# A fused attention and MLP kernel: the prologue's steps in another order, with fewer zero products

## The chip, the cores and the metric

One core of one Trainium2 chip runs the program. The metric is the device time of one execution in microseconds, the median of the runs. The engines are PE (TensorE: matmuls, with the weight loads shown as PEld), DVE (VectorE), ACT (ScalarE), POOL (GpSimd) and SP, whose queue issues the DMAs.

## The reference

Attention over 4 batches, 8 heads, 768 positions and head size 64, in float32: each query sees the 31 keys nearest to it and 24 block summaries (the maximum of 32 keys, the mean of 32 values). Its output, as 3072 rows of 512, goes through a gated MLP with an inner size of 1536.

```python
scores_l = scale * np.matmul(q, k.transpose(0, 1, 3, 2))          # masked to |i - j| < 16
scores_s = scale * np.einsum('bhsd,bhnd->bhsn', q, k_sum) + np.log(32)
a = softmax over both, joined;  out = np.matmul(a, [v, v_sum])
g = x @ w_gate;  val = x @ w_val
return (g / (1 + np.exp(-g))) * val @ w_out
```

The MLP weights arrive as float64, two 32-bit words each.

## The kernel before

The 3072 rows are six blocks of 512 tokens (k = 0 to 5). A block's attention runs over four pairs of heads (u = 0 to 3), its MLP over twelve slices of the inner size (j = 0 to 11). For every float32 product of the MLP each operand is split into a high and a low part that PE multiplies at one pass each, so a slice is three groups of 12 matmuls of 128x512: `gate`, `val` (both line 647) and `down` (line 694).

**The steps.** Attention of (k,u): `sw` and `sp` (block 0) or `scores` (later blocks) are the score products, lines 472, 484 and 458; `ttr0`, `ttr1` take the masked maxima on DVE (line 505, the first half of the heads and the second); `exp0`, `exp1` run on ACT (521); `rcp` and `nrm` normalize (538, 539, 548 or 546); `tr0`, `tr1` turn the probabilities on PE (563); `pt0`, `pt1` copy them out of PSUM; `out` and `outp` multiply by the values (612 and 620); `split` and `rest` make the high and low part of the result (182 and 178). `keys` and `pool` take the block maxima of the keys (336), `pool_values` and `values` bring in the block means of the values (356; on PE the small product pv, line 394).

Weights of slice j (`gv` for gate and value weights together, `o` for the output weights, `g` and `v` apart for j = 0 and 11): `w_load` issues the DMA (201); `w_abs` on ACT (210) and `w_c1`, `w_c2`, `w_s1`, `w_s2` on DVE (215, 219, 227, 234) turn float64 into float32, each reading what the one before it wrote; `w_hi` (182 or 184) and `w_lo` (178) split it. In the MLP: `silu` (653, ACT), `mul` (658, DVE), `ah` (182) and `al` (178) make the split product that `down` reads.

**What sets the order.** The table PROLOGUE lists all 457 steps of block 0 (attention and MLP) and of block 1's attention. The program is built by reading it from the front, and dependencies without a semaphore keep every engine to that order. A step's suffix names its engine (`=a` ACT, `=d` DVE, `=p` POOL) or, for steps on PE, the PSUM pool of its bank (`y`, `g`: two banks each; `c`: four). A digit behind the pool letters asks for that many zero products of 128 columns in that bank ahead of the step (`zeros`, line 740). They change no result, since the step's own first product overwrites the bank. Blocks 2 to 5 and block 1's MLP follow in a loop that is not touched.

**Buffers that order the work.** `gate`, `val` and half of each `scores` share the two `g` banks, so each of them waits until the one two places before it has been read. `pro` holds block 0's tiles; `room(0)` closes it and opens the pools for block 1's tiles and the later weights in its place.

`w_lead` (line 193) shifts the weight tile of one slice by 24 words; `a_max` (line 489) allocates the probabilities when the first half is handled.

Of the kernel before, what the change touches and what calls it, by code (L numbers as in the profile page):

```python
# [100 lines left out]
kf(2) qf(2) qf(0) sw(0,2)=cc pool(2) sp(0,2) kf(0) ttr0(0,2) pool(0) exp0(0,2) ttr1(0,2) exp1(0,2)
sw(0,0)=yg2 sp(0,0) kq(1) kq(3) ttr0(0,0) pool(1) rcp(0,2) nrm(0,2)=p ttr1(0,0) exp0(0,0) w_load(0,g)
sw(0,1)=yg6 sp(0,1) w_load(1,gv) vr() ve() exp1(0,0) ttr0(0,1) vo() tr0(0,2)=c9 ttr1(0,1) rcp(0,0) w_abs(0,g)
exp1(0,1) w_c1(0,g) pool(3) exp0(0,1) w_c2(0,g) w_s1(0,g) w_abs(1,gv) rcp(0,1) tr1(0,2)=g sw(0,3)=cy4 sp(0,3)
ttr0(0,3) nrm(0,0)=p tr0(0,0)=c3 ttr1(0,3) exp0(0,3) exp1(0,3) pt0(0,2)=a w_s2(0,g) w_c1(1,gv) w_c2(1,gv)
rcp(0,3) tr1(0,0)=y nrm(0,1)=p tr0(0,1)=y1 w_s1(1,gv) tr1(0,1)=c nrm(0,3)=d w_s2(1,gv) fv()=g pt1(0,2)=a
w_load(0,v) out(0,2)=c pt0(0,0)=a fvc()=a outp(0,2) pt1(0,0)=a out(0,0)=c tr0(0,3)=c pt0(0,1)=a w_load(0,o)
w_abs(0,v) pt1(0,1)=a w_c1(0,v) w_hi(0,g)=a w_c2(0,v) w_abs(0,o) outp(0,0) tr1(0,3)=y w_lo(0,g)=d w_hi(1,gv)=a
w_s1(0,v) w_load(2,gv) w_c1(0,o) w_s2(0,v) w_load(3,gv) w_lo(1,gv)=d w_c2(0,o) out(0,1)=y split(0,0)=a rest(0,0)
w_s1(0,o) pt0(0,3)=a pt1(0,3)=a outp(0,1) w_abs(2,gv) split(0,1)=a w_load(1,o) cst() w_hi(0,v)=a out(0,3)=g outp(0,3)  # L110
room(0) rest(0,1) gate(0,0,0) split(0,2)=a gate(0,0,1) rest(0,2) gate(0,0,2) split(0,3)=a rest(0,3) w_c1(2,gv)
w_abs(3,gv) gate(0,0,3) gate(0,1) silu(0,0) w_c1(3,gv) w_c2(2,gv) w_s2(0,o) w_lo(0,v)=p w_s1(2,gv) w_c2(3,gv)
w_s2(2,gv) w_abs(1,o) val(0,0,0) val(0,0,1) silu(0,1) w_hi(0,o)=a val(0,0,2) w_s1(3,gv) w_c1(1,o) val(0,0,3)
load(1,0) val(0,1) w_hi(2,gv)=a w_lo(2,gv)=d w_load(2,o) w_c2(1,o) mul(0,0) ah(0,0)=a keys(1,0) gate(0,2)
w_abs(2,o) mul(0,1) w_lo(0,o)=d w_s1(1,o) al(0,0)=d ah(0,1)=a w_s2(3,gv) w_load(3,o) w_load(4,gv) silu(0,2)
scores(1,0) down(0,0) val(0,2) w_s2(1,o) w_hi(3,gv)=a al(0,1)=d ttr0(1,0) pool_values(1,0) ttr1(1,0)
w_lo(3,gv)=p w_abs(4,gv) w_abs(3,o) w_c1(4,gv) w_c1(2,o) w_c2(4,gv) gate(0,3) mul(0,2) val(0,3) w_load(5,gv)
w_s1(4,gv) w_c1(3,o) w_s2(4,gv) exp1(1,0) w_hi(1,o)=a w_c2(3,o) w_lo(1,o)=d exp0(1,0) w_hi(4,gv)=a w_s1(3,o)
w_c2(2,o) w_s2(3,o) w_s1(2,o) w_load(7,gv) w_load(6,gv) rcp(1,0) down(0,1) w_lo(4,gv)=d load(1,1) silu(0,3)
w_abs(5,gv) w_hi(3,o)=a w_c1(5,gv) mul(0,3) gate(0,4) val(0,4) ah(0,2)=a w_abs(7,gv) w_c2(5,gv) w_lo(3,o)=d  # L120
w_s1(5,gv) w_s2(2,o) nrm(1,0)=a w_hi(2,o)=a w_s2(5,gv) al(0,2)=d w_hi(5,gv)=a tr0(1,0) silu(0,4) w_abs(6,gv)
w_load(4,o) tr1(1,0) pt0(1,0)=a w_abs(4,o) w_lo(2,o)=d pt1(1,0)=a down(0,2) keys(1,1) mul(0,4) w_c1(6,gv)
w_lo(5,gv)=d w_c1(4,o) scores(1,1) ah(0,4)=a w_c2(6,gv) ah(0,3)=a ttr0(1,1) exp0(1,1) ttr1(1,1) al(0,4)=d
w_load(5,o) load_values(1,0) w_load(7,o) w_load(6,o) w_c1(7,gv) w_s1(6,gv) values(1,0)=a w_load(9,gv) gate(0,5)
al(0,3)=p w_abs(5,o) w_c2(4,o) w_s2(6,gv) w_load(8,gv) w_s1(4,o) val(0,5) w_c2(7,gv) w_hi(6,gv)=a down(0,3)
out(1,0) silu(0,5) w_lo(6,gv)=d w_s2(4,o) w_c1(5,o) w_s1(7,gv) gate(0,6) w_abs(6,o) mul(0,5) w_hi(4,o)=a
w_lo(4,o)=p down(0,4) pool_values(1,1) w_s2(7,gv) w_c2(5,o) load_values(1,1) exp1(1,1) w_c1(6,o) w_s1(5,o)
w_abs(7,o) w_abs(9,gv) w_c1(9,gv) w_c1(7,o) val(0,6) w_hi(7,gv)=a w_lo(7,gv)=d w_c2(9,gv) split(1,0)=a w_s2(5,o)
rcp(1,1) silu(0,6) w_abs(8,gv) w_c2(6,o) w_s1(9,gv) load(1,2) mul(0,6) rest(1,0) w_hi(5,o)=a w_c2(7,o) ah(0,5)=a
values(1,1)=a al(0,5)=p w_load(8,o) w_load(10,gv) w_s1(6,o) gate(0,7) silu(0,7) nrm(1,1)=a w_load(9,o) val(0,7)  # L130
w_c1(8,gv) w_lo(5,o)=d w_s2(9,gv) w_hi(9,gv)=a tr0(1,1) down(0,5) mul(0,7) ah(0,7)=a pt0(1,1)=a keys(1,2)
scores(1,2) pool_values(1,2) tr1(1,1) w_lo(9,gv)=d w_s2(6,o) w_abs(8,o) w_s1(7,o) gate(0,9) ttr0(1,2) ttr1(1,2)
pt1(1,1)=a w_c2(8,gv) out(1,1) ah(0,6)=a load(1,3) w_hi(6,o)=a w_lo(6,o)=d exp0(1,2) al(0,6)=p w_s2(7,o)
w_c1(8,o) exp1(1,2) w_hi(7,o)=a w_s1(8,gv) al(0,7)=d w_s2(8,gv) w_c2(8,o) val(0,9) down(0,6) w_lo(7,o)=d
w_abs(10,gv) w_abs(9,o) w_c1(9,o) w_hi(8,gv)=a w_c1(10,gv) w_lo(8,gv)=d down(0,7) silu(0,9) rcp(1,2) w_c2(10,gv)
w_s1(10,gv) mul(0,9) split(1,1)=a w_s2(10,gv) w_c2(9,o) nrm(1,2)=a gate(0,8) tr0(1,2) w_hi(10,gv)=a keys(1,3)
w_lo(10,gv)=d w_s1(8,o) val(0,8) ah(0,9)=a rest(1,1) room(1) w_load(11,v) w_load(11,g) silu(0,8) mul(0,8)
load_values(1,2) w_load(10,o) w_load(11,o) w_s2(8,o) pt0(1,2)=a al(0,9)=p w_abs(11,v) ah(0,8)=a w_hi(8,o)=a
w_s1(9,o) al(0,8)=d w_lo(8,o)=d gate(0,10) w_c1(11,v) tr1(1,2) pt1(1,2)=a w_c2(11,v) w_s2(9,o) w_s1(11,v)
w_s2(11,v) scores(1,3) ttr0(1,3) values(1,2)=a w_hi(9,o)=a silu(0,10) down(0,8) ttr1(1,3) val(0,10) w_abs(11,g)  # L140
w_c1(11,g) w_c2(11,g) w_lo(9,o)=p out(1,2) w_s1(11,g) w_s2(11,g) w_abs(10,o) exp1(1,3) w_hi(11,g)=d w_c1(10,o)
w_hi(11,v)=a down(0,9) w_lo(11,g)=p exp0(1,3) split(1,2)=d mul(0,10) w_lo(11,v)=d w_c2(10,o) rcp(1,3) ah(0,10)=a
rest(1,2) gate(0,11) w_abs(11,o) w_c1(11,o) w_c2(11,o) load_values(1,3) nrm(1,3)=a w_s1(10,o) tr0(1,3)
pt0(1,3)=a w_s2(10,o) al(0,10)=d w_hi(10,o)=a silu(0,11) pool_values(1,3) val(0,11) tr1(1,3) pt1(1,3)=a
values(1,3)=a w_s1(11,o) w_lo(10,o)=d down(0,10) w_s2(11,o) out(1,3) w_hi(11,o)=d w_lo(11,o)=p mul(0,11)
# [799 lines left out]
```

## Time and profile before

| | us |
|---|---|
| median of 3 runs | 674.53 (674.50 to 674.58) |
| the profiled execution | 674.72 |
| its span, first to last instruction | 673.0 |
| PE busy | 667.7 |
| DVE, ACT, POOL busy | 340.0, 297.3, 139.6 |
| granted TensorE clock over the span, share of full | 1.00 |

Busy time is the sum over an engine's instructions, and matmuls overlap each other in it; a stretch of PE is therefore better read from the chain of work that ended last, where each piece lasts until the next one starts. The profile's slices show DVE busy nine tenths and more up to some 140 us and a third to a half of the time behind that; PE is busy throughout.

### The profile page before, as it was taken

To read this page: it belongs to the slowest core of one execution; us is meant where nothing else is said; L and a number is where in the kernel's file an instruction comes from. 1 tells how busy PE (TensorE), PEld (TensorE's weight loads), DVE (VectorE), ACT (ScalarE), POOL (GpSimd) and SP (SyncE) were. 2 spreads that over 40 slices of the span, in tenths; PEclk is the share of its full clock that TensorE was granted. 3 is DMA by queue.
4 is the path that set the end of the run, shared out by engine and by line. 5 is a ranking of instruction groups with operands and counts; after the bars stand their busy time and mean duration, and the time that the engine had idled before them with its cause. 6 is when DMAs were issued, how large, how long until landed. Compare 5 with 4: busy or idle time off the path is not lost.

```text
span 673.0 us, 12398 instructions
## 1 busy us (share of the span) xinstructions
PE 667.7 (99%) x4936; PEld 544.0 (81%) x4936; DVE 340.0 (51%) x952; ACT 297.3 (44%) x729; POOL 139.6 (21%) x137
## 2 busy tenths in 40 slices
...
GB/s 336 336 379 345 42 238 171 47 120 135 56 58 0 56 45 122 95 10 79 103 2 168 57 49 82 17 39 65 56 57 57 0 25 0 63 1 0 1 0 64
DMA packets 72059, 60.19 MB, mean 89 GB/s; under 512 B 42272, under 2 KB 60064, under 8 KB 70464
## 3 DMA queue, kind: packets, MB, share of 16 engines
...
q8 instruction: 39, 0.64, 0.4%
...
## 4 chain that ended last, share of the span: by engine, by line
PE 97%; DVE 2%; issue 0%; DVEq 0%
PE g L647 30%; PE v L647 29%; PE acc L694 29%; PE xo L612 4%; PE sc L447 2%; DVE p L505 1%; PE pp L563 1%; PE sc L458 1%; PE xo L620 1%; PE warm L740 0%; DVE ks L336 0%; PE pv L415 0%; PE sc L472 0%; PE end L694 0%; DVE m_g L219 0%
## 5 line engine op out<-in xcount | busy, mean ns | idle before, releaser
L694 PE MATMUL acc<-w_o,ah 128*128 128x512 f32 x572 | 176.2, 389 | 0.0
L647 PE MATMUL g<-xh,w_gv 128*128 128x512 f32 x480 | 159.7, 394 | 0.0
L647 PE MATMUL v<-xh,w_gv 128*128 128x512 f32 x480 | 157.9, 390 | 0.0
L658 DVE TENSOR_TENSOR a<-v,a 128x512 f32<-128x512 f32 x72 | 49.6, 689 | 199.5 <-PE v L647 197.9
L178 POOL TENSOR_TENSOR al<-a,ah 128x512 fp32r<-128x512 f32 x63 | 81.8, 1299 | 328.1 <-ACT ah L182 328.1
L694 PEld LDWEIGHTS acc<-w_o,ah 128*128 128x128 f32 x572 | 107.4, 188 | 22.2
L182 ACT CAST ah<-a 128x512 fp32r<-128x512 f32 x71 | 44.0, 621 | 168.5 <-DVE a L658 168.5
L694 PE MATMUL acc<-w_o,al 128*128 128x512 f32 x286 | 112.0, 392 | 0.0
L647 PEld LDWEIGHTS g<-xh,w_gv 128*128 128x128 f32 x480 | 90.1, 188 | 20.8 <-ACT w_o L182 0.2
L647 PEld LDWEIGHTS v<-xh,w_gv 128*128 128x128 f32 x480 | 90.1, 188 | 18.9
L653 ACT ACTIVATE a<-g 128x512 f32<-128x512 f32 x72 | 43.1, 599 | 134.8 <-PE g L647 131.8
L647 PE MATMUL g<-xl,w_gv 128*128 128x512 f32 x240 | 93.8, 391 | 0.0
L593 DVE STREAM_TRANSPOSE pt_short<-p_short 32x256 f32<-32x256 f32 x192 | 83.8, 436 | 19.8 <-POOL p_short L548 16.9
L647 PE MATMUL v<-xl,w_gv 128*128 128x512 f32 x240 | 93.4, 389 | 0.0
L694 PEld LDWEIGHTS acc<-w_o,al 128*128 128x128 f32 x286 | 53.7, 188 | 11.4 <-DVE al L178 0.2
L647 PEld LDWEIGHTS v<-xl,w_gv 128*128 128x128 f32 x240 | 45.1, 188 | 9.3
L647 PEld LDWEIGHTS g<-xl,w_gv 128*128 128x128 f32 x240 | 45.1, 188 | 8.8
L521 ACT ACTIVATE p_short<-p_short,nm 128x88 f32<-128x88 f32 x128 | 45.3, 355 | 0.2
L178 DVE TENSOR_TENSOR xl<-xo,xh 128x512 fp32r<-128x512 f32 x24 | 16.4, 686 | 56.9 <-ACT xh L182 56.8
L548 POOL TENSOR_TENSOR p_short<-p_short,ri 128x704 f32<-128x704 f32 x16 | 26.0, 1623 | 53.5 <-DVE ri L539 49.6
L647 PE MATMUL g<-xh,w_g 128*128 128x512 f32 x96 | 32.2, 396 | 0.0
L647 PE MATMUL v<-xh,w_v 128*128 128x512 f32 x96 | 31.6, 390 | 0.0
...
## 6 DMA issues: line engine op xcount, KB each, us to landing
...
```

The source lines that it names most:

```text
L178: (nc.vector if e == "d" else nc.gpsimd).tensor_tensor(out=out, in0=a, in1=b.bitcast(F32), op=ALU.subtract)
L182: nc.scalar.copy(out, in_)
L447: nc.tensor.matmul(sc[h][s * SQ : (s + 1) * SQ, c * SC : (c + 1) * SC], t["q"][hs, i * SQ : (i + 1) * SQ], keys[hs], start=True, stop=True,)
L458: nc.tensor.matmul(sc[h][s * QT : (s + 1) * QT, c * KC : (c + 1) * KC], t["q"][hs, qs], t["kw"][hs, i, :], start=True, stop=True,)
L521: nc.scalar.activation(out=t["p"][:, i, :kc], in_=t["p"][:, i, :kc], func=AF.Exp, scale=-1.0, bias=t["nm"][:, i : i + 1], accum_out=t["sm" ...
L548: (nc.vector if on == "d" else nc.gpsimd).tensor_tensor(out=p, in0=p, in1=ri.rearrange("p (n o) -> p n o", o=1).broadcast_to([P, 2 * NTP, ...
L593: nc.vector.transpose(out=to[r * SQ : (r + 1) * SQ, :, s * SQ : (s + 1) * SQ], in_=t["p"][s * SQ : (s + 1) * SQ, :, at : at + SQ],)
L612: nc.tensor.matmul(ps[hs, qs], vw, t["pt"][:n, h, qs], start=k not in OWN or i == 0, stop=k not in OWN)
L647: nc.tensor.matmul(ps, w[:, cs], x, start=u == 0 and n == 0, stop=u == NP - 1 and n == 2)
L653: nc.scalar.activation(out=a, in_=A.pop(("g", k, j)), func=AF.Silu)
L658: nc.vector.tensor_tensor(out=a, in0=ps, in1=a, op=ALU.mult)
L694: nc.tensor.matmul(out, a[:, ts], w[:, cs], start=begin and n == 0, stop=end and n == 2)
```

## The change

From the 75th step on (382 of the 457) the table has another order. Ahead of that only zero counts differ: `sw(0,0)` 2 to 5, `sw(0,1)` 6 to 3, `tr0(0,2)` 9 to 6, `sw(0,3)` 4 to 1, `tr0(0,0)` 3 to none; `tr0(0,1)` keeps its one. That is 16 zero products of 128 columns for 25.

Engines change too. From DVE to POOL go nine subtractions: `w_lo` of (1,gv), (2,gv), (6,gv), (0,o), (5,o), (8,o), (10,o) and `al` of slices 4 and 11. From POOL to DVE go six: `w_lo` of (3,gv), (0,v), (11,o) and `al` of 3, 6 and 9. The casts `w_hi` of (0,g), (9,o) and (11,v) go from ACT to DVE, `ah(0,11)` the other way. `tr1(0,3)`, `out(0,1)` and `out(0,3)` take banks of other pools. In the new table `ttr1` stands ahead of `ttr0` for some pairs, for which `a_max` now allocates by who comes first; the shift of 24 words goes from the value weights of slice 11 to its gate weights. The new digits that `a_far` accepts are used by no step.

```diff
-tr0(0,1)=y1 tr1(0,1)=c ... out(0,0)=c tr0(0,3)=c pt0(0,1)=a ... outp(0,0) tr1(0,3)=y w_lo(0,g)=d w_hi(1,gv)=a
+tr0(0,1)=y1 tr1(0,1)=c ... out(0,0)=c tr0(0,3)=c pt0(0,1)=a tr1(0,3)=c w_abs(0,v) w_load(0,o) outp(0,0) w_hi(0,g)=d
...
     def w_lead(j, nm):
-        return LEAD if (nm, j) == ("v", NJ - 1) else 0
+        return LEAD if (nm, j) == ("g", NJ - 1) else 0
...
     def a_far(k, u):
         t = U[k, u]
         m = P if on[:1] == "h" else QT
+        for _ in range(int(on) if on.isdigit() else 0):
+            nc.tensor.matmul(t["sc"][0][:, NTP * KC :], warm[:, :P], warm[:, : TOK - NTP * KC], start=True, stop=True)
...
-        if g == 0 and k >= SHORT:
+        first = "p" not in t
+        if first and k >= SHORT:
             t["p"] = short["p"]
-        elif g == 0:
+        elif first:
             t["p"] = (two if k else pro).tile([P, 2 * NTP, KC], F32, tag="p", bufs=1 if k else 4, name=f"p_{k}_{u}")
-        if g == 0:
+        if first:
```

On PE, the end of block 0's attention, before. `pp0` and `pp1` are the two turns, `xo` the products with the values, of the block and pair in the name; `g_0_0` is the first MLP product:

```order
L612 MATMUL xo_0_0_484<-pt_0_0_475,vrows_283 64x64 x16
L563 MATMUL pp0_0_3_501<-consts_104,p_0_3_372 120x128 x4
L620 MATMUL xo_0_0_484<-pt_0_0_475,vs_0_114 64x512 x2
L563 MATMUL pp1_0_3_521<-consts_104,p_0_3_372 120x128 x4
L612 MATMUL xo_0_1_538<-pt_0_1_506,vrows_283 64x64 x16
L620 MATMUL xo_0_1_538<-pt_0_1_506,vs_0_114 64x512 x2
L612 MATMUL xo_0_3_575<-pt_0_3_560,vrows_283 64x64 x16
```

The same place in the changed kernel:

```order
L615 MATMUL xo_0_0_482<-pt_0_0_473,vrows_283 64x64 x16
L566 MATMUL pp0_0_3_499<-consts_104,p_0_3_371 120x128 x4
L566 MATMUL pp1_0_3_506<-consts_104,p_0_3_371 120x128 x4
L623 MATMUL xo_0_0_482<-pt_0_0_473,vs_0_114 64x512 x2
L615 MATMUL xo_0_1_524<-pt_0_1_504,vrows_283 64x64 x16
L623 MATMUL xo_0_1_524<-pt_0_1_504,vs_0_114 64x512 x2
L615 MATMUL xo_0_3_560<-pt_0_3_541,vrows_283 64x64 x16
```

The two turns of pair 3 now stand together, ahead of pair 0's last product with the values.

On PE, behind block 1's scores of pair 2 (`sc0`, `sc1`, whose last two products are shown), before:

```order
L458 MATMUL sc0_1_2_1295<-kw_1_2_1202,q_1_2_1199 64x120
L458 MATMUL sc1_1_2_1296<-kw_1_2_1202,q_1_2_1199 64x120
L563 MATMUL pp1_1_1_1315<-consts_104,p_1_1_1009 120x128 x4
L647 MATMUL g_0_9_1325<-xh_0_0_555,w_gv9_1267 128x512
L647 MATMUL g_0_9_1325<-xl_0_0_556,w_gv9_1267 128x512
```

and in the changed kernel:

```order
L458 MATMUL sc0_1_2_1308<-kw_1_2_1259,q_1_2_1256 64x120
L458 MATMUL sc1_1_2_1309<-kw_1_2_1259,q_1_2_1256 64x120
L615 MATMUL xo_1_1_1336<-pt_1_1_1273,vw_1_1_963 64x64 x16
L650 MATMUL g_0_9_1356<-xh_0_0_550,w_gv9_1271 128x512
L650 MATMUL g_0_9_1356<-xl_0_0_551,w_gv9_1271 128x512
```

The products of pair 1 with the values follow the scores directly; before, they stood by themselves behind `gate(0,9)`. The turn that stood here goes ahead of the scores.

On POOL, from the first weight subtraction on, before (`kw` are small copies of key maxima):

```order
L178 TENSOR_TENSOR w_v0_573<-m_v0_510,w_v0_573 128x512
L184 COPY kw_1_0_674<-ks_0_169 128x4x24
L184 COPY kw_1_0_674<-ks_0_702 128x4x24
L178 TENSOR_TENSOR w_gv3_782<-m_gv3_621,w_gv3_782 128x1024
L184 COPY kw_1_1_882<-ks_1_230 128x4x24
```

and in the changed kernel:

```order
L178 TENSOR_TENSOR w_gv1_548<-m_gv1_327,w_gv1_548 128x1024
L184 COPY kw_1_0_659<-ks_0_169 128x4x24
L184 COPY kw_1_0_659<-ks_0_687 128x4x24
L178 TENSOR_TENSOR w_gv2_715<-m_gv2_597,w_gv2_715 128x1024
L178 TENSOR_TENSOR w_o0_674<-m_o0_522,w_o0_674 128x512
```

POOL now makes the low parts of the gate and value weights of slices 1 and 2 and of the first output weights.

## Rows read from the trace of the kernel before

**Rows 1.** The page: busy us (share of the span) and instructions of each engine

```profile
PE 667.7 (99%) x4936; PEld 544.0 (81%) x4936; DVE 340.0 (51%) x952; ACT 297.3 (44%) x729; POOL 139.6 (21%) x137
```

**Rows 2.** Chain that ended last, 0 to 60 us: start us, us, what

```profile
25.08 0.95 PE xo L612 x32
26.02 0.58 PE pp L563 x4
...
28.20 1.08 PE xo L612 x32
...
31.94 5.66 PE g L647 x24
...
45.76 0.98 PE sc L458 x32
46.74 2.99 PE acc L694 x12
```

**Rows 3.** The same chain, 58 to 152 us

```profile
79.15 1.08 PE xo L612 x32
80.23 2.94 PE g L647 x12
83.17 2.72 PE acc L694 x12
...
98.37 0.58 PE pp L563 x4
...
113.90 0.44 PE pp L563 x4
114.34 2.75 PE v L647 x12
```

**Rows 4.** Timeline of PE, 0 to 32 us: start, us, what [idle before, releaser]

```profile
1.53 3.35 PE L740 MATMUL warm<-warm 128*128 128x512 f32 x4 [1.53 <-DVE warm L816]
4.92 1.56 PE L472 MATMUL sc<-kq 64*64 64x96 f32 x32
...
7.19 0.85 PE L740 MATMUL sc<-warm 128*128 128x256 f32 x2
...
9.24 0.66 PE L484 MATMUL sc<-ks,kq 64*64 64x24 f32 x32 [0.21 <-DVE ks L336]
9.84 1.56 PE L740 MATMUL sc<-warm 128*128 128x512 f32 x4
11.32 0.89 PE L472 MATMUL sc<-kq 64*64 64x96 f32 x32
...
19.83 0.46 PE L740 MATMUL pp<-warm 128*128 128x128 f32 x2 [0.35 <-DVE nm L505]
```

**Rows 5.** Timeline of DVE, 0 to 46 us

```profile
9.96 0.28 DVE L505 CUSTOM_DVE_ANT_0 p<-sc,bias 128x120 f32<-128x120 f32 x1
...
15.87 1.15 DVE L219 TENSOR_SCALAR m_g<-m_g 128x512 int32<-128x512 int32 x1
...
25.93 0.43 DVE L215 TENSOR_SCALAR m_v<-m_v 128x512 f32<-128x512 f32 x1 [0.40 <-ACT m_v L210]
26.39 0.43 DVE L219 TENSOR_SCALAR m_v<-m_v 128x512 int32<-128x512 int32 x1
...
40.41 1.21 DVE L178 TENSOR_TENSOR w_gv<-m_gv,w_gv 128x1024 fp32r<-128x1024 f32 x1
41.54 0.41 DVE L219 TENSOR_SCALAR m_o<-m_o 128x512 int32<-128x512 int32 x1
41.88 0.68 DVE L658 TENSOR_TENSOR a<-v,a 128x512 f32<-128x512 f32 x1
42.48 0.94 DVE L336 TENSOR_REDUCE ks<-kt 128x24 f32<-128x768 f32 x1
```

**Rows 6.** Timeline of ACT, 0 to 46 us

```profile
39.10 1.05 ACT L182 CAST w_gv<-m_gv 128x1024 fp32r<-128x1024 f32 x1 [0.36 <-DVE m_gv L234]
```

**Rows 7.** Timeline of POOL, 46 to 52 us

```profile
48.12 2.42 POOL L178 TENSOR_TENSOR w_gv<-m_gv,w_gv 128x1024 fp32r<-128x1024 f32 x1 [4.37 <-ACT w_gv L182]
```

More of the change, by code (lines that the diff above doesn't have):

```diff
@@ L100 @@
 PROLOGUE = """
[L101 to L145, printed above, removed]
@@ new lines @@
+w_lo(1,gv)=p outp(0,3) room(0) rest(0,0) w_load(2,gv) gate(0,0,0) split(0,1)=a w_abs(2,gv) rest(0,2) w_load(1,o)
+w_load(3,gv) w_hi(0,v)=a rest(0,1) w_s1(0,o) gate(0,0,1) w_c1(2,gv) split(0,3)=a gate(0,0,2) w_s2(0,o)
+w_abs(3,gv) rest(0,3) w_abs(1,o) gate(0,0,3) gate(0,1) silu(0,0) w_load(2,o) w_lo(0,v)=d w_c2(2,gv) w_c1(3,gv)
+w_s1(2,gv) val(0,0,0) silu(0,1) load(1,0) load_values(1,0) val(0,0,2) val(0,0,1) w_c2(3,gv) w_hi(0,o)=a
+w_s2(2,gv) w_load(5,gv) w_load(4,gv) w_abs(2,o) w_load(3,o) w_s1(3,gv) keys(1,0) val(0,0,3) w_s2(3,gv) mul(0,0)
@@ new lines @@
+pool_values(1,0) w_load(9,gv) val(0,1) mul(0,1) w_load(6,gv) w_hi(2,gv)=a w_hi(3,gv)=a scores(1,0) ah(0,0)=a
+w_abs(5,gv) ttr1(1,0) w_abs(4,gv) w_lo(2,gv)=p ttr0(1,0) w_abs(3,o) values(1,0)=a w_c1(2,o) w_load(5,o)
+w_c1(1,o) w_lo(0,o)=p gate(0,2) w_c2(2,o) w_c1(4,gv) w_load(6,o) val(0,2) w_c2(1,o) w_c2(4,gv) al(0,0)=d
+down(0,0) w_lo(3,gv)=d silu(0,2) exp0(1,0) exp1(1,0) w_s1(1,o) gate(0,3) mul(0,2) w_s1(2,o) w_s2(1,o)
+w_load(8,gv) w_s1(4,gv) load(1,1) ah(0,1)=a w_c1(3,o) w_c1(5,gv) w_hi(1,o)=a w_s2(4,gv) w_abs(6,gv) w_load(7,gv)
@@ new lines @@
+scores(1,1) out(1,0) w_s2(6,gv) w_lo(3,o)=d w_abs(5,o) down(0,2) split(1,0)=a w_hi(6,gv)=a w_lo(6,gv)=p
+w_c2(7,gv) w_s1(7,gv) ah(0,4)=a w_c2(4,o) al(0,4)=p silu(0,5) w_s2(7,gv) ttr1(1,1) w_hi(7,gv)=a ttr0(1,1)
+exp0(1,1) exp1(1,1) down(0,3) rest(1,0) pool_values(1,1) val(0,5) gate(0,6) mul(0,5) silu(0,6) w_load(10,o)
+w_lo(7,gv)=d w_c1(6,o) w_s1(4,o) w_c1(5,o) w_s2(4,o) w_abs(8,gv) w_c2(6,o) w_c2(9,gv) w_s1(6,o) val(0,6)
+w_hi(4,o)=a w_s2(6,o) rcp(1,1) mul(0,6) w_lo(4,o)=p w_hi(6,o)=a ah(0,6)=a w_c2(5,o) w_c1(8,gv) gate(0,7)
```

32 lines of the change are left out of this document (31 added, 1 removed).

## The prediction

> **What bounds the kernel now.** I read the page first: PE is busy 99% of the span [rows 1]. That alone proves little, since matmuls overlap, so the second view was the chain of work that ended last. The reader is to see two things in it. From 31.94 us, the first MLP product, it runs through PE without a break, and a group of 12 matmuls in the middle of the prologue takes 2.72 us (83.17 [rows 3]), 0.227 each, where 512 columns at 2.4 GHz need 0.213: hardly anything stretches it. Ahead of that, third view, PE's timeline shows only 0.21 and 0.35 us of idle time behind DVE [rows 4], because zero products fill the waits. There the chain lies on DVE's maxima and jumps to PE at 19.83. So some 20 us of start hang on DVE, ACT and POOL, and everything behind is PE's own work. In the sections from 20 to 140 us DVE and ACT only have to be in time.
>
> The Trainium skill (Perfetto Trace Analysis, Identifying the Most-Contended Engine) calls matmul busy time a bad measure and wants the share of LDWEIGHTS instead, 81% here. By it up to a fifth of PE's time could be hidden slack, and a better order could win microseconds; the trace does not agree, since 0.227 against 0.213 leaves 6% at most [rows 3], and the loads of the next weights lie in it.
>
> **The change, part by part.** The sum is made against the profiled execution, 674.72 us with a span of 673.0; that execution lies 0.19 above the median of 674.53, and I apply the differences to the median.
>
> *Zero products.* Nine fewer. Six units took 1.48 us from 9.84 to the next piece at 11.32, 0.25 each [rows 4], so 2.2 us of PE work goes. It is worth nothing as such: the removed ones lie between 9.84 and 19.83, where PE then waits for POOL and DVE anyway. `tr0(0,1)` keeps its unit, and the wait of 0.35 in front of it is for DVE's maxima [rows 4], whose order is unchanged. What counts is the one place that gets more: `sw(0,0)`, three units or 0.74 us ahead of pair 0's scores. PE stood 0.21 there for the key maxima [rows 4], and DVE took up these scores at 9.96 [rows 5], 0.06 behind their end at 9.90. So DVE's run of maxima may slip by 0.74 - 0.21 - 0.06 = 0.47 us, and with it all up to 19.83; at the other end, where ACT, which reads the maxima, has slack, nothing. I take +0.2 (0 to +0.5).
>
> *The two turns of pair 3 together.* Before: 0.58 + 0.58 for the turns and 1.08 for the products with the values behind the second one [rows 2]. After: the second turn follows its like, 0.44 as behind big matmuls [rows 3], and `xo` follows `xo`, 0.95 as at 25.08 [rows 2]. That is 2.24 against 0.58 + 0.44 + 0.95 = 1.97, or -0.27, if pair 3's copy out of PSUM comes as much earlier; its place on ACT hardly moves (one cast leaves ahead of it, one `split` enters), so I take -0.2 (-0.27 to 0).
>
> *Block 1's attention between the MLP groups.* The MLP group behind an attention piece pays for the switch: 2.94 behind `xo`, 2.99 behind scores, 2.75 behind a turn, against 2.72 [rows 2, 3], or 0.22, 0.27 and 0.03. Going through both tables, block 1's attention enters the MLP stream at 14 places before and 10 after. Those that end in scores fall from 1 to 0, in `xo` from 4 to 3, in turns from 5 to 3; those that end in pv stay 4. Saved: 0.27 + 0.22 + 0.06 = 0.55. One turn no longer follows scores (0.58 against 0.44 [rows 3]): 0.14 more. Two `xo` now follow scores, which no row shows; from below 0.95 as behind its like, from above 1.08 + 0.14, so -0.13 to +0.14 each, and I take none, being nearest to 1.08 behind turns and big matmuls alike [rows 2, 3]. One pv behind `xo` costs 0 to 0.14; I take 0.05. Together -0.64 (-0.95 to -0.27).
>
> *DVE, ACT and POOL.* Priced from start to start, a subtraction of 512 costs DVE 0.60 (41.88 to 42.48), of 1024 1.13 (40.41 to 41.54), a cast 0.34 (41.54 to 41.88) [rows 5]. Nine subtractions leave DVE (three of 1024): 6.99. Six come: 4.13. Three casts come and one of 0.60 leaves: +0.42. Net -2.4 us of some 115. A step right behind the one it reads starts 0.46 after it (25.93 to 26.39) instead of 0.34 [rows 5]; of such neighbours in the weight chains I count 12 in the old order and 10 in the new one, 0.24 us. None of this is on the path, as PE does not wait for DVE behind 20 us: cost and gain nothing. PE's own work is the cover; where a result comes late, it costs the lateness (below).
>
> *DMA.* `w_load(2,o)` moves ahead of block 1's first loads on SP's queue, `load_values(1,0)` ahead of the weights of slices 4 and 5, which come later by its 0.4 MB. Their first readers on ACT had slack; I take nothing, and leave the price to the second rival. The 24 words of `w_lead` only move an address: nothing.
>
> Sum: +0.2 - 0.2 - 0.64 = -0.64, so 673.9 us. The bounds add up to -1.2 and +0.2 without lateness.
>
> **The rivals.** *PE's clock falls, slower.* The first near scores took 1.56 us for 32 products and the same 32 at 11.32 0.89 [rows 4]: PE began at the lower level (1.2 GHz) and reached the upper one (2.4) in or ahead of the zero products at 7.19. Twelve units fewer behind 9.84 leave some 2.9 us of new idle time up to 19.83. If the level falls there, the stretch behind 20 us runs at half speed as the first one did, from 1.53 to about 7.2 [rows 4]: some 5.7 us of low level, half of it lost, +2.8. That gives 676.7. It decides from the point where PE's waits are long enough to lose the level. For it: the zeros are there for no other use. Against: the longest single wait I can place is the last one, behind the first turns of pair 0, about 2 us, and PE works in between. The Trainium skill (TensorE: Matmul & The Clock Gate, The HAM clock gate) says that the clock is halved by default and that idle time takes it back; by that rule this rival would come true, and the trace shows only its rising side.
>
> *An operand comes late.* Two tight places. `down(0,1)` reads `al(0,1)`: from `mul(0,0)`, if it starts at 41.88 as before [rows 5], DVE has 24 steps of 15.4 us up to the end of `al(0,1)`, 57.3; PE comes there at 31.94 + 5.66 + 2 x 2.72 = 43.04 [rows 2, 3], plus 1.2 for scores and pv, plus 5 x 2.72, or 57.8. And `gate(0,2)` reads a low part that POOL now makes: its high part was done on ACT at 39.10 + 1.05 [rows 6], the subtraction takes 2.42 [rows 7], so 42.6 with nothing ahead of it, against PE's 44.2. A POOL product in DVE's way costs too: the same operation took 1.15 at 15.87 and 0.43 at 26.39 [rows 5], so 0.7 may go at each of three more POOL subtractions. The Trainium skill (GPSIMD Engine Reference, Key points) tells the same of their shared SBUF interfaces; it speaks against moving work to POOL. A stall is paid once, since it gives every later step slack: 0.3 to 1.5 us, so 674.2 to 675.4.
>
> *More is won.* All bounds at their best end give 673.3; to pass 0.2% (1.35 us, 673.2, about what a measurement can tell from no change) some wait must go that the profile hides, such as a stretch of `xo` and `outp` between 20 and 32 us. 672.9.
>
> *The change does not do what it says.* Neighbours fall only from 12 to 10, and if DVE's stretch grows by what POOL takes, PE sees neither: 674.5, inside the forecast's range.
>
> **How the numbers follow.** The forecast 673.9 gets 0.55, no effect at all (674.5) 0.12, late operands 0.15, the fallen clock 0.07, more won 0.11. Lateness passes the upper bound of 675.9 (1.35 above 674.53) seldom, 0.03, so slower has 0.10; faster by over 0.2% takes the rival's 0.11 and 0.02 of the forecast's lower tail, 0.13; within 0.2% remains 0.77. The range runs from 673.0, below the best sum of the bounds, to 675.3, which holds nearly all of the late operands; it leaves out the clock, the worst of the lateness and the better half of what more might be won, under 2 in 10.
>
> **What would show it.** Right: the first MLP product starts within 0.4 us of 31.94; up to 144 us the chain stays on PE; 12-matmul groups stay at 2.72, with ten attention places between them, and `down(0,11)` ends 0.3 to 1 us sooner. The clock: turns and `xo` behind 20 us twice as long. Late operands: idle time of PE in front of `gate(0,2)` or `down(0,1)`, with POOL or DVE as releaser. Wrong altogether: a first MLP product over 1 us away from 31.94, or PE idle behind 20 us for over 1 us.

## The result, and the profile after

The changed kernel takes 682.44 us (median of 4 runs, 681.22 to 683.41) against 674.51 us before: a ratio of 1.0116, 95% interval 1.0099 to 1.0134. I had forecast 673.9 us. The profiled execution took 683.41 us with a span of 681.6, so 8.6 us of span have to be found. Of the four runs it alone has a mean granted clock of 0.995; the one at 1.000 took 681.22 us, so most of the loss is not the clock.

The page of the changed kernel has hardly moved against [rows 1]: PE 2.2 us more, GpSimd 8.6 us more, VectorE and ScalarE as before. Busy time does not show the loss.

```profile
PE 669.9 (98%) x4932; PEld 545.7 (80%) x4932; DVE 339.6 (50%) x951; ACT 296.6 (44%) x727; POOL 148.2 (22%) x140
```

Two landmarks on PE's timeline cut the span in three: the first MLP product, and the last `xo` of the prologue, `xo(1,3)`. They stand at 31.87 and 140.07 us before and at 33.39 and 148.74 after. So the start lost 1.5 us, the stretch between them 7.15 (108.20 to 115.35), and the rest nothing (532.93 and 532.86). I use the same cut for every kernel below.

*The start.* PE's timeline of the changed kernel, 16 to 34 us (start, us, engine, line, operation, then idle time before it and its releaser); it answers to [rows 4] and [rows 2]:

```profile
16.90 1.09 PE L566 MATMUL pp<-consts,p 128*120 128x128 f32 x8
19.93 0.57 PE L743 MATMUL pp<-warm 128*128 128x128 f32 x2 [1.94 <-DVE nm L508]
20.30 1.91 PE L566 MATMUL pp<-consts,p 128*120 128x128 f32 x8
22.14 2.53 PE L415 MATMUL pv<-vrows,mean 128*32 128x128 f32 x56
...
33.39 0.50 PE L650 MATMUL g<-xh,w_g 128*128 128x512 f32 x1
```

VectorE releases PE at the same time as before, 19.9 us, but the products that stood in front of this wait are gone: 0.35 us of idle time became 1.94. Behind it the eight turns take 1.91 us. The windows of the same trace say why (stretch; its length; busy us of PE, its weight loads, VectorE, ScalarE, GpSimd; granted clock; DMA share; GB/s):

```profile
20.00:24.00 4.00, 4.00 (x54) 3.56 (x58) 3.93 (x7) 3.23 (x13) 0.14 (x1) 0.57 1.01 405
24.00:28.00 4.00, 4.00 (x92) 2.94 (x85) 2.47 (x5) 3.20 (x9) 0.00 (x0) 1.00 1.04 417
```

A granted clock of 0.57 is mostly the lower of the two levels, 1.2 GHz. It was 1.00 in this stretch before. The Trainium skill (TensorE: Matmul & The Clock Gate, The HAM clock gate) says that the halved clock is the default and that idle time brings it back; here the trace agrees, with 0.57 behind 1.94 us of idle time.

*The stretch.* Most of the loss lies between 119 and 146 us. Three views belong together. SyncE's queue, first before, then after: the three loads of the last weight slice (`raw_v`, `raw_g`, `raw_o` of slice 11). The last row before merges two loads: `raw_o` of slice 10 at 110.93 and that of slice 11 at 115.82.

```profile
101.28 0.34 SPq L201 DMA_DIRECT2D raw_v<-in_wends  x1
109.55 0.33 SPq L201 DMA_DIRECT2D raw_g<-in_wends  x1
109.98 0.90 SPq L329 DMA_DIRECT2D vw<-in_vP  x2
110.93 5.24 SPq L201 DMA_DIRECT2D raw_o<-in_wo  x2
```

```profile
104.28 0.88 SPq L329 DMA_DIRECT2D vw<-in_vP  x2
117.99 0.35 SPq L201 DMA_DIRECT2D raw_g<-in_wends  x1
118.40 0.42 SPq L201 DMA_DIRECT2D raw_v<-in_wends  x1
118.87 0.42 SPq L201 DMA_DIRECT2D raw_o<-in_wo  x1
```

ScalarE and PE of the changed kernel, 116 to 130 us:

```profile
121.73 0.66 ACT L210 ACTIVATE m_g<-raw_g 128x512 f32<-128x512 f32 x1 [4.18 <-DMA raw_g<-in_wends]
122.29 0.57 ACT L182 COPY pt<-pp 120x512 f32<-120x512 f32 x1
```

```profile
118.93 0.60 PE L566 MATMUL pp<-consts,p 128*120 128x128 f32 x4
119.46 1.05 PE L458 MATMUL sc<-kw,q 64*64 64x120 f32 x32
122.92 0.39 PE L394 MATMUL pv<-consts,vr 128*24 128x128 f32 x1 [2.40 <-ACT pt L182]
127.19 0.60 PE L566 MATMUL pp<-consts,p 128*120 128x128 f32 x4
128.98 0.47 PE L650 MATMUL v<-xh,w_gv 128*128 128x512 f32 x1 [1.19 <-DVE nm L508]
```

The load lands at 121.7, 3.7 us after its issue. ScalarE works in order: `w_abs(11,g)` waits for the load, and the copy `pt1(1,2)`, whose turn PE had done at 119.5, stands behind it. PE stood for 2.40 us, and lost the clock again:

```profile
123.00:126.00 3.00, 3.00 (x8) 2.42 (x9) 0.95 (x1) 2.89 (x6) 1.28 (x1) 0.51 0.20 79
```

Then `val(0,10)` waited 1.19 us for VectorE. Smaller waits stand at 68.44 (0.16), at 79.98 (0.36, `val(0,5)` behind `ttr1(1,1)`) and at 145.43 (0.20).

*Why the loads are late.* No wait was written for this. The weights of slices 0 to 10 are decoded in three buffers of the pool `dec`; each tile takes the buffer that was freed first. `room(1)` closes the pool, and the three tiles of slice 11 lie in its place, in the order in which they are loaded. In the new order `w_abs(5,gv)` stands ahead of `w_abs(4,gv)` and `w_abs(6,gv)` ahead of `w_abs(7,gv)`, and the buffers rotate differently. Byte addresses in a partition, as built:

| tile | before | changed |
|---|---|---|
| `w_gv(9)` decoded at | 217056 | 221152 |
| `w_gv(8)` decoded at | 221152 | 225248 |
| `w_gv(10)` decoded at, freed last | 225248 | **217056** |
| first load of slice 11, from | 216864 | 216864 |
| second | 221056 | 221056 |
| third | 225152 | 225152 |

Each decode buffer is 4096 bytes long. The first load now lies over the buffer that is freed last, the second reaches into it by 96 bytes, and the third, whose place was long free, queues behind them on SyncE. Before, the third load lay over that buffer, and it alone went out as late, at 115.82.

### The profile page after: what moved, and what is told of

Read it like the earlier page. It is cut to its first block, busy times and chain, and to the rows that moved or that the text cites. A ratio compares the mean times of both kernels' runs of the same rounds, so it can differ in the third digit from the quotient of the medians.

```text
span 681.6 us, 12397 instructions
## 1 busy us (share of the span) xinstructions
PE 669.9 (98%) x4932; PEld 545.7 (80%) x4932; DVE 339.6 (50%) x951; ACT 296.6 (44%) x727; POOL 148.2 (22%) x140
## 4 chain that ended last, share of the span: by engine, by line
PE 88%; issue 4%; DVE 4%; ACT 1%; DMA 1%; POOL 1%; SPq 0%; POOLq 0%; ACTq 0%
PE g L650 27%; PE v L650 27%; PE acc L697 26%; PE xo L615 3%; PE sc L447 2%; DVE p L508 1%; DMA kq<-in_kF 1%; PE pp L566 1%; POOL w_o L178 1%; PE xo L623 1%; DVE ks L336 0%; ACT p L524 0%; ACT L524 0%; PE pv L415 0%; DVE m_gv L227 0%
## 5 line engine op out<-in xcount | busy, mean ns | idle before, releaser
L178 POOL TENSOR_TENSOR al<-a,ah 128x512 fp32r<-128x512 f32 x62 | 80.2, 1294 | 318.1 <-ACT ah L182 318.1
L650 PEld LDWEIGHTS g<-xh,w_gv 128*128 128x128 f32 x480 | 90.8, 189 | 21.4 <-ACT a L656 0.4
L184 POOL COPY kw<-ks 128x384 f32<-128x384 f32 (+2 forms) x28 | 14.8, 530 | 89.5 <-DVE ks L336 63.3
```

The lines of the kernel that those rows point to most:

```text
L178: (nc.vector if e == "d" else nc.gpsimd).tensor_tensor(out=out, in0=a, in1=b.bitcast(F32), op=ALU.subtract)
L184: (nc.vector if e == "d" else nc.gpsimd).tensor_copy(out, in_)
L650: nc.tensor.matmul(ps, w[:, cs], x, start=u == 0 and n == 0, stop=u == NP - 1 and n == 2)
```

## The experiments

Medians, ratios and landmarks of all runs; "rest" is the span behind `xo(1,3)`. Kernels whose name begins with "before" are edits of the kernel before, the others of the changed one. The cuts of the table PROLOGUE show the steps that moved; the rest of each line is left out.

| kernel | us | ratio to before (95%) | first MLP product | stretch | rest |
|---|---|---|---|---|---|
| before | 674.5 | | 31.87 | 108.20 | 532.93 |
| changed | 682.44 | 1.0099 to 1.0134 | 33.39 | 115.35 | 532.86 |
| loads_apart | 680.70 | 1.0071 to 1.0099 | 33.01 | 111.43 | 534.56 |
| zeros_back | 682.33 | 1.0092 to 1.0128 | 33.32 | 114.06 | 532.92 |
| both_back | 680.26 | 1.0067 to 1.0093 | 31.36 | 112.65 | 534.59 |
| before_few_zeros | 676.28 | 1.0009 to 1.0033 | 33.20 | 108.20 | 533.10 |
| thirds | 678.18 | 1.0042 to 1.0077 | 31.89 | 111.79 | 532.92 |
| before_moved | 676.68 | 1.0017 to 1.0039 | 32.06 | 108.36 | 534.58 |
| turns_early | 677.75 | 1.0029 to 1.0059 | 33.17 | 110.37 | 532.96 |
| three_places | 680.54 | 1.0067 to 1.0103 | 31.68 | 112.50 | 532.92 |
| three_dve | 681.15 | 1.0080 to 1.0108 | 33.18 | 113.49 | 532.93 |
| before_thirds | 675.32 | 1.0002 to 1.0021 | 31.66 | 108.71 | 532.93 |
| turns_zeros | 677.01 | 1.0019 to 1.0044 | 31.30 | 111.36 | 532.94 |
| abs_behind | 679.46 | 1.0055 to 1.0089 | 32.92 | 112.48 | 532.60 |

### The late loads: loads_apart, thirds, before_thirds, abs_behind

**loads_apart** lays slice 11's tiles out as o, g, v at the first of their loads, 48 words up.

```diff
-LEAD = 24
+LEAD = 48
-        return LEAD if (nm, j) == ("g", NJ - 1) else 0
+        return LEAD if (nm, j) == ("o", NJ - 1) else 0
...
+        for x in "ogv" if j == NJ - 1 and (nm, j) not in raw else (nm,):
+            if (x, j) not in raw:
+                raw[x, j] = w_pool(j).tile([P, w_lead(j, x) + 2 * n], I32, tag=f"{x}{j}", name=f"raw_{x}{j}")
+        w = raw[nm, j][:, w_lead(j, nm) :]
```

> The changed kernel, with the three weight tiles of step 11 laid so that only w_o(11) lies on the third of the buffers in which w_gv(10) is still decoded; the order of all steps is the change's own. Theory L (the loss behind 119 us comes from the three loads, issued at 118 us behind the decoding of weights 10): SP issues raw_g and raw_v before 111 us, the wait of pv for pt of 2.40 us and the 1.19 us of v behind it are gone, the granted clock stays 1.00 from 120 to 140 us, and the time falls from 682.4 to between 676 and 678. Rival O (the order of turns, exponentials and multiplications there is slow in itself, and the late loads only go with it): the loads come early as well, but PE still waits for over 2 us between 119 and 150 us, and the time stays over 680.5.

The stretch fell by 3.92 us and PE's wait at `pv` was gone, as theory L had it; the 1.19 us at `val(0,10)`, which it had going too, stayed. The time fell by only 1.7, since the rest grew by 1.7 (below): 680.70 us is over L's range and just over rival O's bound of 680.5, but of the 2 us and more that O had for PE's waits between 119 and 150 us 1.38 are there.

**thirds** exchanges the decode buffers instead and leaves slice 11 where it was.

```diff
+THIRD = {"0g": 2, "1gv": 0, "0v": 1, "2gv": 2, "3gv": 0, "5gv": 1, "4gv": 2, "6gv": 0, "7gv": 2, "9gv": 1, "8gv": 0, "10gv": 2}
-            m = dec.tile([P, len(nm) * DM], F32, tag="m", name=f"m_{nm}{j}")
+            x = THIRD[f"{j}{nm}"]
+            m = dec.tile([P, 2 * DM], F32, tag=f"m{x}", bufs=1, name=f"m_{nm}{j}")[:, : len(nm) * DM]
```

> The changed kernel with the lowest and the highest of the three decode buffers exchanged, so that w_gv(10) is decoded in the highest and only the last of the three loads of step 11 has to wait for it; the weights of step 11 stay where the changed kernel has them (loads_apart had moved them by 96 bytes and more). Theory L with place (the loads are worth 3.9 us, as the stretch from the first MLP product to the last down, 116.43 us in the changed kernel and 112.51 us in loads_apart, shows; loads_apart gave 1.65 us of it back behind 150 us because step 11's weights stood at other addresses): 678.3 to 679.3. Rival (the addresses cost nothing and loads_apart is all that the loads give): 680.2 to 680.9.

678.18 us, just under the range of theory L and 4.3 under the changed kernel. Some of that is the start: PE stood for 1.94 us at 19.91 in this execution too, but did not lose its clock there (granted 1.00 from 20 to 24 us), so 1.5 of its 5.0 us of span stand in the first landmark, and 3.56 in the stretch. Between the runs at a mean granted clock of 1.000 it is 2.9 to 3.3 us (677.92 to 678.31 against 681.22). The largest single part of the loss was one choice of a buffer. SyncE of thirds:

```profile
106.12 0.35 SPq L202 DMA_DIRECT2D raw_g<-in_wends  x1
106.52 0.42 SPq L202 DMA_DIRECT2D raw_v<-in_wends  x1
116.81 0.33 SPq L202 DMA_DIRECT2D raw_o<-in_wo  x1
```

**before_thirds** makes the same exchange in the kernel before, to its harm.

> The kernel before, all steps in its own order, with the lowest and the highest decode buffer exchanged the other way: w_gv(10) is now decoded in the lowest, under the first of the three loads of step 11. Theory L in the mirror: SP issues raw_v behind the decoding of w_gv(10), at 115.8 us instead of 101.28, with raw_g and raw_o queued behind it; it lands about 3.7 us later, the rectifying of w_v(11) holds ScalarE from 115.9 to 119.5 us ahead of ah(0,8), w_hi(8,o) and pt1(1,2), PE waits at pv or at down(0,8), and the time is 676.0 to 678.5. Rival (the loads have slack, and the order of the changed kernel alone makes them matter): under 675.2.

The loads went out as late as expected, `raw_v` at 115.59, and cost 0.7 us; PE waited 0.3 us at `pv`. At 675.32 us the run lies between the two, just above the rival's bound. A late load is not dear in itself.

**abs_behind** leaves the changed kernel's loads late and moves one ScalarE step.

```diff
-w_load(11,o) w_s1(9,o) w_abs(11,g) pt1(1,2)=a
-w_s2(9,o) w_hi(8,o)=a pool_values(1,3) scores(1,3) ttr1(1,3) values(1,2)=a gate(0,10)
+w_load(11,o) w_s1(9,o) pt1(1,2)=a
+w_s2(9,o) w_hi(8,o)=a pool_values(1,3) scores(1,3) ttr1(1,3) values(1,2)=a w_abs(11,g) gate(0,10)
```

> The changed kernel with one step moved on ScalarE: the rectifying of w_g(11), which waits for the late load, stands behind pt1(1,2), w_hi(8,o) and the values of pair 2 instead of ahead of them; the loads stay as late as the changed kernel has them (issued at 118 us, landed at 121.7). Theory Q (the late load costs PE only through ScalarE's order: the copy pt1(1,2) is ready at 119.2 us and stands behind a step that waits for the load until 121.73; in the kernel before_thirds the load was as late and cost 0.7 us, since the steps behind it there had room): the 2.40 us of pv and most of the fall of the clock behind it are gone, and the time is 679 to 680.3. Rival (the load is needed that early by VectorE too, whose w_c1(11,g) stands ahead of ttr0(1,3), and val(0,10) then waits as long): 681 or more.

Theory Q held: 679.46 us, 3.0 less, with the loads at 118.57 us; the runs at a mean granted clock of 1.000 are 678.00 and 681.22. ScalarE's copy `pt1(1,2)` and PE's `pv` in this kernel:

```profile
120.11 0.58 ACT L182 COPY pt<-pp 120x512 f32<-120x512 f32 x1 [1.98 <-PE pp L566]
```

```profile
120.98 0.28 PE L394 MATMUL pv<-consts,vr 128*24 128x128 f32 x1
```

The copy follows its turn at once, and PE does not wait. So the late load did most of its harm through one step ahead of `pt1(1,2)` on an engine that works in order.

### The start: zeros_back, before_few_zeros, both_back

All three exchange the counts of zero products.

```diff
-sw(0,0)=yg5
+sw(0,0)=yg2
...
-sw(0,1)=yg3
+sw(0,1)=yg6
...
-tr0(0,2)=c6
+tr0(0,2)=c9
...
-sw(0,3)=cy1
+sw(0,3)=cy4
...
-tr0(0,0)=c
+tr0(0,0)=c3
```

**before_few_zeros** is the other direction, in the kernel before.

> The kernel before with the zero products of the changed one (5, 3, 6, 1 and none instead of 2, 6, 9, 4 and 3); nothing else. Theory Z: PE stands for 1.3 us or more ahead of the turn at 19.8 us (0.35 now, with 0.9 us of zero products taken out ahead of it), the granted clock falls behind it, the first MLP product comes at 33.0 to 33.6 instead of 31.94, and the time is 675.6 to 676.3. Rival (my forecast of nothing from these products): within 0.5 us of 674.5.

PE's timeline and a window of it:

```profile
19.66 0.46 PE L740 MATMUL pp<-warm 128*128 128x128 f32 x2 [1.94 <-DVE nm L505]
19.96 1.51 PE L563 MATMUL pp<-consts,p 128*120 128x128 f32 x8
21.40 3.03 PE L415 MATMUL pv<-vrows,mean 128*32 128x128 f32 x56
```

```profile
20.00:24.00 4.00, 4.00 (x58) 3.24 (x56) 3.93 (x7) 2.97 (x12) 0.00 (x0) 0.57 1.02 414
```

Theory Z held: the same 1.94 us, the same 0.57, 676.28 us. The runs show a choice of two: in eight of ten the mean granted clock of the whole run was 0.997, seven of them at 676.14 to 676.37 and one at 679.04; in two it was 1.000, at 674.23 and 674.96. Of the 15 runs of the kernel before beside them one had 0.997, and 676.73 us. So the nine products that looked idle buy 1.7 us whenever the level would have fallen.

**zeros_back** puts them back in the changed kernel.

> The changed kernel with the zero products of the kernel before (2, 6, 9, 4 and 3 instead of 5, 3, 6, 1 and none); nothing else. Theory Z (PE stood 1.94 us at 19.93 us because the products that stood there are gone, and the granted clock of 0.57 followed from that): the idle time ahead of the turn at 19.9 us is under 0.6 us, the granted clock from 20 to 24 us is 1.00, the first MLP product is within 0.4 us of 31.94 (33.39 in the changed kernel), and the time is 680.5 to 681.4, 1.0 to 1.9 less. Rival D (VectorE comes later there by the order, and zero products only fill the wait): the first MLP product stays over 33 us and the time over 681.8.

It gained nothing (682.33), and in the traced execution the start was as late, for another reason:

```profile
6.28 0.70 PE L743 MATMUL sc<-warm 128*128 128x256 f32 x2
8.73 1.56 PE L472 MATMUL sc<-kq 64*64 64x96 f32 x32 [1.75 <-DMA kq<-in_kF]
```

A first load of keys landed at 8.7 us here, where the two zero products ended at 7.0; the next products ran at 1.2 GHz (granted clock 0.50 from 9 to 12 us; 1.56 us instead of 0.89). The changed kernel's five at this place cover most of such a wait. In both_back and before_thirds PE stood there for 1.01 and 1.21 us, and the same products took 0.89. So this execution neither confirms nor refutes what the wait at 19.9 costs (PE comes to that place at 21.4 us here and waits 0.23); both_back and turns_zeros do.

It puts a price on the second fall, though. PE stood for 2.50 us at `pv` here too, but the granted clock stayed at 1.00 from 123 to 126 us, and the stretch is 1.29 us shorter than the changed kernel's. So some 1.3 of its 7.15 us are the clock behind the late load and not the wait itself.

**both_back** is loads_apart with these counts.

> The changed kernel with both edits: weight tiles of step 11 apart, zero products as before. Theory L and Z together: what is left of the change is the new order of 382 steps, with 0.5 us of waits seen between 68 and 80 us and the 0.64 us that fewer switches between attention and MLP were to give; 673.7 to 675.2, a ratio of 0.999 to 1.001 to the kernel before. Rival O: the order has losses of its own behind 119 us, over 676.5.

The start came back, 31.36 us, but of these 1.65 us the stretch gave back 1.22, and the time fell by 0.4 only. The sum of theory L and Z was refuted, also without the 1.65 us that the place of the weights costs (below): the order of the steps costs something itself.

### What the order costs: turns_early, three_places, three_dve, turns_zeros

In thirds PE still waits at `val(0,10)`. VectorE and PE there:

```profile
122.87 0.28 DVE L510 CUSTOM_DVE_ANT_0 p<-sc,bias 128x120 f32<-128x120 f32 x1 [2.38 <-ACT ah L183]
```

```profile
122.12 0.60 PE L568 MATMUL pp<-consts,p 128*120 128x128 f32 x4
123.91 0.47 PE L652 MATMUL v<-xh,w_gv 128*128 128x512 f32 x1 [1.19 <-DVE nm L510]
```

The trace puts VectorE's 2.38 us down to ScalarE, in the changed kernel (3.64 us) to PE's `pp`. The second is right: pair 3's maxima write `p`, of which there is one buffer in block 1, and pair 2's `p` is read until `tr0(1,2)`, the `pp` at 122.12. The new order has `ttr1(1,3)` ahead of `tr0(1,2)`, which stands behind `gate(0,10)` on PE; and `val(0,10)` needs the bank that `ttr1(1,3)` frees. **turns_early** moves that turn.

```diff
-down(0,7) tr1(1,2) w_load(11,v)
+down(0,7) tr1(1,2) tr0(1,2) w_load(11,v)
...
-pt1(1,2)=a w_s2(9,o)
+pt1(1,2)=a pt0(1,2)=a w_s2(9,o)
...
-w_lo(8,o)=p tr0(1,2) w_lo(9,o)=p val(0,10) pt0(1,2)=a w_c1(10,o)
+w_lo(8,o)=p w_lo(9,o)=p val(0,10) w_c1(10,o)
```

> The kernel thirds with one step moved: tr0(1,2), which stands behind gate(0,10), stands directly behind tr1(1,2), with its copy pt0(1,2) behind pt1(1,2). Theory P (ttr1(1,3) writes the one buffer p that tr0(1,2) still reads, so VectorE stands from 121.25 to 123.63 us until PE has come past gate(0,10), and val(0,10) then waits 1.19 us for the bank that ttr1(1,3) frees): VectorE's wait of 2.4 us is under 0.8, the 1.19 us of val(0,10) is gone, at most 0.5 us is given back at the scores or at pv, and the time is 0.8 to 1.4 us under thirds. Rival (VectorE is late there anyway by its queue of weight steps): within 0.4 us of thirds.

VectorE's wait and the 1.19 us are gone, 0.28 us came back at the scores, and the stretch fell by 1.42. The median fell by 0.4 only, since three of its four runs had a mean granted clock of 0.997 and of thirds' one; the runs at 1.000 are 677.08 against 677.92 to 678.31. Theory P is right on the mechanism; on the time, by medians, the run lies between the two.

**three_places** takes the two other waits away in the same manner.

```diff
-w_c2(7,gv) w_s1(7,gv) ah(0,4)=a w_c2(4,o) al(0,4)=p silu(0,5) w_s2(7,gv) ttr1(1,1) w_hi(7,gv)=a
+w_c2(7,gv) ttr1(1,1) w_s1(7,gv) ah(0,4)=a w_c2(4,o) al(0,4)=p silu(0,5) w_s2(7,gv) w_hi(7,gv)=a
...
-w_c2(11,o) al(0,10)=d gate(0,11) split(1,2)=d val(0,11) rest(1,2)
+w_c2(11,o) split(1,2)=d rest(1,2) al(0,10)=d gate(0,11) val(0,11)
```

> The kernel turns_early with two more moves: ttr1(1,1) stands four VectorE steps earlier (ahead of w_s1(7,gv)), and split(1,2) and rest(1,2) stand ahead of al(0,10). Theory P for all waits that are left on PE: the 0.59 us of val(0,5) at 79 us and the 0.9 us between tr1(1,3) and tr0(1,3) at 140 us go too, and the time is 2.0 to 2.7 us under thirds, near 676.4. Rival (each wait that goes opens one behind it): less than 1.5 us under thirds.

It lost 2.8 us by the medians, 1.7 between the runs at 1.000. VectorE, GpSimd and PE of this kernel, 76 to 90 us:

```profile
76.78 2.64 DVE L221 TENSOR_SCALAR m_o<-m_o 128x512 int32<-128x512 int32 x1
79.34 2.31 DVE L236 SCALAR_TENSOR_TENSOR m_gv<-raw_gv,m_gv 128x1024 int32<-128x1024 int32 x1
```

```profile
76.55 2.58 POOL L179 TENSOR_TENSOR w_gv<-m_gv,w_gv 128x1024 fp32r<-128x1024 f32 x1 [8.12 <-ACT w_gv L183]
79.10 1.48 POOL L179 TENSOR_TENSOR al<-a,ah 128x512 fp32r<-128x512 f32 x1
```

```profile
84.58 0.50 PE L652 MATMUL v<-xh,w_gv 128*128 128x512 f32 x1 [1.12 <-DVE a L663]
89.15 0.50 PE L652 MATMUL g<-xh,w_gv 128*128 128x512 f32 x1 [1.54 <-ACT a L658]
```

The step that takes VectorE 0.42 us in thirds took 2.64, until GpSimd's subtraction was done; the next waited for GpSimd's second one. The earlier `ttr1(1,1)` had made VectorE 0.23 us later than GpSimd. In thirds GpSimd started last and took 3.35 us. Both fit one reading: neither is slowed in part; the one that starts second is held until the other is done. The Trainium skill (SBUF — State Buffer, Who interferes with whom) says just that: the pair of ports that VectorE and GpSimd share is an exclusive lock, and the order of issue decides who blocks. The trace agrees, with 2.64 us against 0.42.

**three_dve** takes GpSimd out of it.

```diff
-w_lo(6,gv)=p
+w_lo(6,gv)=d
```

> The kernel three_places with one subtraction, w_lo(6,gv), on VectorE instead of GpSimd. In three_places GpSimd's subtraction of 2.58 us at 76.55 us ran beside two VectorE steps that took 2.64 us (0.42 elsewhere) and 2.31 us (1.22 elsewhere), and PE then waited 1.12 and 1.54 us. Theory S (the two engines slow each other there): both steps have their usual lengths, VectorE is net 2 us earlier at 82 us, PE's waits between 80 and 90 us fall under 0.6 us in sum, and the time is 676 to 677.2. Rival (the earlier ttr1(1,1) itself pushes the weights of step 7 too late): PE still waits over 1.5 us between 80 and 90 us, over 678.5.

The step of 0.42 us had its length again (0.41 at 82.61), but the subtraction now made VectorE wait 2.15 us for ScalarE's cast, `al(0,4)` on GpSimd held another step (1.78 us instead of 0.68), and PE waited 2.29 us at 87.08. Theory S told the mechanism, its rival the outcome: with `ttr1(1,1)` early the weights of slice 7 come too late. I found no place for it that costs nothing.

**turns_zeros** gathers what had helped: thirds, turns_early, the later of three_places' two moves, and the old zero products with five in the first group.

> The kernel turns_early, with split(1,2) and rest(1,2) ahead of al(0,10) as in three_places (but ttr1(1,1) in the changed kernel's place), and with the zero products of the kernel before except the first group, which keeps the changed kernel's 5: that one covers a first load that landed late in zeros_back. The causes found so far undone together: loads 3.9 us, val(0,10) 1.4, the turns of pair 3 0.5, and the fall of the clock at the start 1.7 where it comes. First MLP product at 31.3 to 32.0 us, granted clock 1.00 from 20 to 32 us, 675.8 to 676.8. Rival Z2 (the wait at the first turns comes back at another place): first MLP product over 32.8 us, over 677.3.

The start came at 31.30 us, with a granted clock of 1.00 behind 20 us, and the time is 677.01 us, just over the range. PE's waits behind it, 36 to 146 us:

```profile
50.09 0.50 PE L699 MATMUL acc<-w_o,al 128*128 128x512 f32 x1 [0.70 <-DVE al L179]
58.73 0.47 PE L699 MATMUL acc<-w_o,al 128*128 128x512 f32 x1 [0.19 <-DVE al L179]
67.81 0.50 PE L652 MATMUL g<-xh,w_gv 128*128 128x512 f32 x1 [0.23 <-ACT a L658]
...
119.76 1.05 PE L460 MATMUL sc<-kw,q 64*64 64x120 f32 x32 [0.29 <-issue]
142.66 1.15 PE L617 MATMUL xo<-pt,vw 120*64 120x64 f32 x32 [0.26 <-ACT pt L183]
```

With 0.54 at 79.54 that is 2.2 us of waits, and the kernel is 2.4 over the kernel before, which has none there. An earlier start shows them: PE gains on VectorE, and the new order has no slack left between 40 and 80 us. Against turns_early the start is 1.87 us earlier and the stretch 0.99 longer. In the kernel before the slack is there: before_few_zeros starts 1.33 later and its stretch is the same 108.20.

### Where the weights stand: before_moved

The rest of loads_apart grew by 1.7 us, though no step there had changed. **before_moved** moves slice 11's weights in the kernel before by 96 bytes.

```diff
-LEAD = 24
+LEAD = 48
```

> The kernel before with 48 words ahead of step 11's weights instead of 24: they stand 96 bytes further up, the order of all steps is untouched. Theory of place: the products with w_g(11), w_v(11) and w_o(11) take 3 to 5 ns more each behind 150 us, as in loads_apart, and the time is 675.8 to 676.4. Rival (what loads_apart lost behind 150 us has another cause): within 0.4 us of 674.6.

676.68 us, 1.9 more, and the rest grew by the same 1.65. Three rows of PE's timeline, before and then before_moved: the first product with `w_g(11)` in block 1, the first with `w_v(11)`, and the first that follows.

```profile
238.87 0.39 PE L647 MATMUL g<-xh,w_g 128*128 128x512 f32 x1
241.59 0.39 PE L647 MATMUL v<-xh,w_v 128*128 128x512 f32 x1
244.31 0.39 PE L694 MATMUL acc<-w_o,al 128*128 128x512 f32 x1
```

```profile
239.32 0.39 PE L647 MATMUL g<-xh,w_g 128*128 128x512 f32 x1
242.12 0.40 PE L647 MATMUL v<-xh,w_v 128*128 128x512 f32 x1
244.93 0.39 PE L694 MATMUL acc<-w_o,al 128*128 128x512 f32 x1
```

A group of twelve takes 2.80 to 2.81 us instead of 2.72: each product with slice 11's gate and value weights takes 7 to 8 ns longer. Those with slice 0's, which have the same names in the profile, do not (`gate` of slice 0 from 249.09 to 251.99 before, from 249.74 to 252.63 moved). Why the address matters was not tried.

No version here beats the kernel before.

## Why the prediction was wrong, step by step

- *What bounds the kernel.* Right for the kernel before. I read from it that VectorE and ScalarE "only have to be in time" and then priced them at nothing, without laying the new order's due times beside PE's. The 2.4 us less that I had computed for VectorE show as 0.4 less busy time (339.6 against 340.0), and five results came late in the changed kernel all the same.
- *"DMA: I take nothing", and "the 24 words of `w_lead` only move an address: nothing".* The step that failed most: 3.56 us of the stretch, some 1.3 of them for the clock that fell behind the wait. I looked at the queue's order and not at what each load overwrites. The lead itself did nothing (the rest is 532.9 in both kernels); what counted was which buffer `w_gv(10)` got. The sentence was false in another way too: an address can cost time, 1.65 us in before_moved.
- *The clock, 0.07 and 676.7.* It came true. The wait I could place, "about 2 us", was 1.94; I took PE's work in between for enough to hold the level. The size was too large: 1.33 us in the first landmark and 1.65 in the median, where I had 2.8, because 20 to 24 us ran low and not 5.7 us. It then fell a second time, behind the wait at 122.9, which I had not thought of.
- *An operand comes late, 0.15 and 0.3 to 1.5 us.* The right rival with the wrong places and a bound too small. `gate(0,2)` never waited. Once the start was early (turns_zeros), `down(0,1)` did, 0.19 us, and ahead of it `down(0,0)`, 0.70 us. The places were `pt1(1,2)` behind a load, `val(0,10)` behind a buffer of `p` (1.4 us), `val(0,5)`, and `tr0(1,3)`. "A stall is paid once, since it gives every later step slack" failed too: the waits at 122.9 and 128.98 stood one behind the other.
- *Zero products, +0.2.* "It is worth nothing as such" is what failed: with them gone PE's wait of 0.35 us became 1.94, the clock fell behind it in most executions, and the kernel before without them takes 1.65 us more (before_few_zeros). Of the one price I gave, for the first group, 0.1 us at most shows: VectorE released the last turns at 19.93 us instead of 19.83.
- *Neighbours and switches, -0.64.* Not won. Take loads_apart: its stretch is 3.23 over the kernel before. From the start of the turns to the next product, 1.80 us at 122.88 instead of 0.36, 0.98 instead of 0.23 from the last product ahead of `val(0,5)` to that one (79.60), and 1.24 instead of 0.35 at 139.89 make 3.1 of it, so some 0.15 is left where I had -0.64. I had booked the switches of the MLP products only. A turn in front of scores takes 0.53 (118.93 to 119.46 in the changed kernel), one in front of MLP 0.36 (113.74 to 114.10 before); there are three of the former now and one before. And a pv behind scores took 0.30 (45.10 to 45.40) where it took 0.04 before (70.68 to 70.72). That is 0.6, as much as I had booked to be saved.
- *The two turns of pair 3, -0.2.* In part: the eight turns take 1.05 us (27.53 to 28.58 in the changed kernel) instead of twice 0.58 [rows 2].

By its own test the prediction was "wrong altogether": the first MLP product lay 1.5 us away, and PE stood for 4.3 us behind 20 us.

What stays open: some 0.2 us of the stretch, and why the clock's level falls in eight of ten executions behind the same wait and not in the other two, and behind the 2.40 us at `pv` in the changed kernel and not behind the 2.50 in zeros_back. Only one execution of each kernel was traced; of the others the mean granted clock is known and not where it fell.
